# Softmax row sums taken from ScalarE's exponentials instead of from the product with the values, with one reciprocal on VectorE for two steps

## The chip, the cores and the metric

The kernel runs on one core of one Trainium2 chip. The core has five engines that work side by side, each through its own instructions in order: TensorE (PE in the profile; PEld is its loading of weights), VectorE (DVE), ScalarE (ACT), GpSimd (POOL) and SyncE (SP), which here only issues transfers. The metric is the device time of one execution in microseconds (us), smaller is better.

## What is computed

64 heads of attention (8 batches, 8 heads, 576 rows, 64 columns) in which every query keeps only its 32 largest scores, followed by a feed-forward layer with a squared ReLU on 4,608 rows of 512.

```python
scores = scale * (q @ k.T)                       # per head, 576 x 576
kth    = the 32nd largest score of each row
scores = where(scores >= kth, scores, -1e9) - max(row)
attn   = exp(scores) / (sum(exp(scores)) + 1e-9)
x      = attn @ v                                # heads side by side: 4608 x 512
h      = maximum(x @ w_in, 0)                    # 4608 x 2048
out    = (h * h) @ w_out                         # 4608 x 512
```

The sum in the denominator is what this change is about.

## The kernel before

The attention is cut into `U = 144` steps. A step `u` treats two blocks of 128 query rows (`x = 0, 1`), each against all 576 keys of its head. The loop over `u` is a software pipeline written out by hand: every instruction is pinned, so each engine runs them in the order in which the loop names them. In one pass of the loop the work of several steps is mixed:

- GpSimd finishes step `u-1`: `drop` (L409) makes a byte per score that tells whether it lies under the 32nd largest, and a transfer (L413) adds these bytes, read as huge negative numbers, to the scores `s`.
- VectorE finds the 32 largest of step `u`: `quads_of` (L323, L324), then four rounds of MAX8 (L374) with MATCH_REPLACE8 (L378) between them, and between the rounds `pairs_of(u+1)` (L314, L315), which opens the next step. Between rounds 0 and 1 stands `invert(u-4)`, a reciprocal (L475).
- TensorE makes the scores of step `u+1` (L285, banks `sc_a` and `sc_b`), the products with the values of step `u-4` (`weigh`, L461, bank `av_ps`) and pieces of the feed-forward (L579, L630).
- ScalarE, in this order: two copies of the scores of `u+1` out of PSUM (`s`, L294); now and then preparation of a coming pair of heads (L175, L213 to L225); `place(u-4)` (L494, L499), which scales the two product blocks by the reciprocals; `exps(u-2)` (L417), two exponentials of 128 x 576, with the row's maximum as bias, into `w_two`; `copy_far(u+1)` (L330); a part of the feed-forward (L586, L594 and others); and `negate(u)` (L394), which waits for the last round of MAX8 and gives GpSimd its threshold.
- SyncE transposes `w_two` with a transfer (`turn`, L426), after both exponentials of the step.

The sums come with the products: the value tile `va` has a 65th column that is all ones, so column 64 of `av_ps` is the row's sum of the weights, and `invert` reads two of them (one for each `x`) straight from PSUM. `sums(u)` gives that bank; the last two steps, 142 and 143, have banks of their own, and step 143 and half of step 142 take their weights from VectorE's `mask` and not from `exps`. Behind the loop stands the tail, which finishes steps 140 to 143 and the rest of the feed-forward.

`copy_far` and `quads_of` both touch the tile `most`; in the built program L323 of a step waits for ScalarE's L330 of the same step, and L314 waits for the second of ScalarE's two copies.

Of the kernel before, what the change touches and what calls it, by code (L numbers as in the profile page):

```python
# [13 lines left out]
f32 = mybir.dt.float32  # L14
# [4 lines left out]
AF = mybir.ActivationFunctionType  # L19
# [4 lines left out]
def kernel(  # L24
# [9 lines left out]
    nc = tc.nc  # L34
    B, H, S, D = q.shape
# [9 lines left out]
    def pin(ins):  # L45
        tc.keep_in_program_order(ins)
        return ins
# [6 lines left out]
    small = fast.enter_context(tc.tile_pool(name="small", bufs=2))  # L54
# [21 lines left out]
    w_two = [const.tile([128, 2, S], bf16, name=f"w_two_{i}") for i in "abc"]  # L76
# [185 lines left out]
    U = len(steps)  # L262
# [6 lines left out]
    st = {}  # L269
# [144 lines left out]

    def exps(u, x):
        d = st[u]
        pin(nc.scalar.activation(w_two[u % 3][:, x, 0:S], d["s"][:, x, :], AF.Exp, bias=d["neg"][:, x, 0:1]))  # L417

    def mask(u, x):
        d = st[u]  # L420
# [45 lines left out]
    def sums(u):  # L466
        if u < U - 2:
            return av
        if u not in last_two:
            last_two[u] = bank(u - (U - 2), [128, 512], f32)  # L470
        return last_two[u][:, 0:130].rearrange("p (x d) -> p x d", x=2)

    def invert(u):
        r = small.tile([128, 2, 1], f32, name="rsum", bufs=4)
        pin(nc.vector.reciprocal(r[:, :, :], sums(u)[:, :, 64:65]))  # L475
        st[u]["r"] = r
# [284 lines left out]
    def finish(w):  # L761
        if ok(w):
            invert(w)
            place(w)
# [11 lines left out]
    for u in range(U):  # L776
# [20 lines left out]
        if ok(u - 4):  # L797
            invert(u - 4)
# [11 lines left out]
        if ok(u - 2):  # L810
            exps(u - 2, 0)
            exps(u - 2, 1)
            turn(u - 2)
        fetch(4 if u < 12 else 3)
        if u == U - 1:
            early_exps(u, 0)
            early_exps(u, 1)
            exps(u - 1, 0)
# [42 lines left out]
    for x in range(2):  # L861
        turn_by_tensor(U - 1, x)
        turned(U - 1, x, False)
    one.square()
    invert(U - 4)
    place(U - 4)
    two.relu()
# [165 lines left out]
```

## Time and profile before

| | |
|---|---|
| median of 3 runs (904.73 to 907.03) | 905.09 us |
| time of the profiled execution | 905.09 us |
| its span, first to last instruction | 903.0 us |
| VectorE busy | 881.8 us, 98% |
| GpSimd busy | 779.0 us, 86% |
| ScalarE busy | 760.1 us, 84% |
| TensorE busy | 678.7 us, 75% |

The profiled execution's own time is the median itself; 2.1 us of it lie outside the span. A group of instructions is given with its line, engine, operation, output and inputs, count, busy time, mean duration of one, and the idle time of the engine before it with what ended that. Durations of neighbours on one engine overlap (the next starts before the end of the one ahead is recorded), so what an instruction takes from its engine is read from start to start. In a timeline the columns are start, duration, engine, line, operation and tiles, count, and in brackets the idle time of the engine before it and what ended that.

### The profile page before, as it was taken

To read this page: it belongs to the slowest core of one execution; us is meant where nothing else is said; L and a number is where in the kernel's file an instruction comes from. 1 tells how busy PE (TensorE), PEld (TensorE's weight loads), DVE (VectorE), ACT (ScalarE), POOL (GpSimd) and SP (SyncE) were. 2 spreads that over 40 slices of the span, in tenths; PEclk is the share of its full clock that TensorE was granted. 3 is DMA by queue.
4 is the path that set the end of the run, shared out by engine and by line. 5 is a ranking of instruction groups with operands and counts; after the bars stand their busy time and mean duration, and the time that the engine had idled before them with its cause. 6 is when DMAs were issued, how large, how long until landed. Compare 5 with 4: busy or idle time off the path is not lost.

```text
span 903.0 us, 21007 instructions
## 1 busy us (share of the span) xinstructions
PE 678.7 (75%) x6274; PEld 424.6 (47%) x6274; DVE 881.8 (98%) x3635; ACT 760.1 (84%) x1752; POOL 779.0 (86%) x818
## 2 busy tenths in 40 slices
PE   5777777777777777767687777677777777887796
PEld 3334454445444445444454444444444444554455
DVE  6999999999999999999999999999999999999995
ACT  3566799889988898888988899988999888997883
POOL 7999988988988888898898888998898988899880
PEclk9989999999999999999999999998999999999999
DMA  6699989899999999899899999999899999687762
GB/s 147 106 155 207 179 186 191 192 197 203 194 193 184 199 190 197 190 192 210 186 201 185 195 194 191 199 196 191 189 206 186 209 202 214 145 162 181 158 142 53
DMA packets 290778, 164.78 MB, mean 182 GB/s; under 512 B 258145, under 2 KB 268641, under 8 KB 290657
## 3 DMA queue, kind: packets, MB, share of 16 engines
q1 hardware_dynamic: 267408, 80.29, 48.0%
q0 software_dynamic: 21904, 82.65, 40.6%
q8 instruction: 52, 0.85, 0.4%
q14 instruction: 70, 0.57, 0.2%
q10 hardware_dynamic: 1344, 0.43, 0.2%
HBM read 37.75 MB, written 9.44 MB: 52 GB/s over the span
## 4 chain that ended last, share of the span: by engine, by line
DVE 74%; issue 12%; ACT 5%; PE 4%; DMA 2%; POOL 2%; SPq 0%; POOLq 0%; DVEq 0%; ACTq 0%
DVE m L374 31%; DVE cat L378 20%; DVE sc_b L314 6%; DVE most L315 5%; DVE cat L324 5%; DVE cat L323 5%; ACT s L294 1%; DVE rsum L475 1%; DMA s<-gone_b 1%; ACT rl L586 1%; DMA s<-gone_a 1%; POOL cat L347 1%; PE dn_ps L630 1%; PE sc_b L285 1%; ACT x_tok L494 0%
## 5 line engine op out<-in xcount | busy, mean ns | idle before, releaser
L374 DVE MAX8 m<-cat 128x8 f32<-128x104 f32 (+3 forms) x1152 | 435.4, 416 | 0.0
L378 DVE MATCH_REPLACE8 cat<-m,cat 128x104 f32<-128x104 f32 (+2 forms) x864 | 260.7, 306 | 0.0
L338 POOL TENSOR_TENSOR cat<-s 128x576 int32<-128x576 int32 (+1 forms) x144 | 238.6, 1657 | 2.7 <-ACT s L294 2.7
L347 POOL TENSOR_TENSOR cat<-cat,most 128x576 int32<-128x576 int32 (+1 forms) x144 | 196.1, 1362 | 25.0 <-DVE m L374 7.5
L285 PE MATMUL sc_b<-qkT 64*128 64x288 f32 x512 | 107.4, 494 | 88.4 <-DVE cat L324 84.2
L285 PE MATMUL sc_a<-qkT 64*128 64x288 f32 x512 | 97.3, 453 | 95.4 <-DVE most L315 39.2
L579 PEld LDWEIGHTS <-w_in 128*128 128x128 bf16 x2304 | 146.2, 101 | 38.6 <-issue 15.7
L630 PE MATMUL dn_ps<-w_out,h 128*128 128x512 bf16 x560 | 159.5, 416 | 0.3 <-ACT h L594 0.3
L579 PE MATMUL gen<-xT,w_in 128*128 128x128 bf16 x2016 | 137.1, 224 | 2.2 <-ACT xT L538 1.4
L409 POOL TENSOR_SCALAR gone_a<-s,neg 128x576 uint8<-128x576 f32 x143 | 107.1, 749 | 16.0 <-ACT neg L394 4.8
L409 POOL TENSOR_SCALAR gone_b<-s,neg 128x576 uint8<-128x576 f32 x142 | 106.3, 749 | 12.6 <-ACT neg L394 0.9
L294 ACT ACTIVATE s<-sc_b 128x576 f32<-128x576 f32 x144 | 93.4, 648 | 25.4 <-PE sc_b L285 21.5
L285 PEld LDWEIGHTS sc_a<-qkT 64*128 64x128 f32 x512 | 41.4, 186 | 123.4 <-issue 33.3
L294 ACT ACTIVATE s<-sc_a 128x576 f32<-128x576 f32 x144 | 91.3, 634 | 4.9 <-PE sc_a L285 3.2
L285 PEld LDWEIGHTS sc_b<-qkT 64*128 64x128 f32 x512 | 43.9, 198 | 103.8 <-PE av_ps L461 63.5
L394 ACT ACTIVATE neg<-m 128x4 f32<-128x4 f32 (+1 forms) x145 | 29.9, 206 | 70.6 <-DVE m L374 69.6
L594 ACT ACTIVATE h<-rl 128x512 bf16<-128x512 f32 x136 | 85.7, 630 | 4.3
L586 ACT ACTIVATE rl<-gen 128x512 f32<-128x512 f32 x142 | 83.0, 586 | 0.7 <-PE gen L579 0.6
L630 PEld LDWEIGHTS <-h 128*128 128x128 bf16 x560 | 53.3, 104 | 61.6 <-issue 26.3
L461 PEld LDWEIGHTS <-wT 128*128 128x128 bf16 (+1 forms) x1600 | 54.5, 100 | 54.4 <-issue 43.9
L413 POOL DMA_DIRECT2D s<-gone_b x67 | 59.3, 885 | 22.0 <-DVE m L374 9.0
L413 POOL DMA_DIRECT2D s<-gone_a x66 | 58.3, 884 | 20.4 <-DVE m L374 12.0
(172 smaller groups left out, 1248.6 us busy)
## 6 DMA issues: line engine op xcount, KB each, us to landing
s<-gone_b POOLq DMA_DIRECT2D x67, 576.0 KB, 4.6
s<-gone_a POOLq DMA_DIRECT2D x66, 576.0 KB, 4.8
v_raw<-in_v_dram SPq DMA_DIRECT2D x64, 128.0 KB, 3.3
k_raw<-in_k_dram SPq DMA_DIRECT2D x63, 128.0 KB, 3.4
q_raw<-in_q_dram SPq DMA_DIRECT2D x63, 128.0 KB, 3.2
out_dram<-wide SPq DMA_DIRECT2D x31, 256.0 KB, 3.0
v_raw<-in_v_dram SPq DMA_DIRECT2D x64, 32.0 KB, 3.0
w_in<-in_moe_w_in_dram POOLq DMA_DIRECT2D x8, 256.0 KB, 4.7
```

The source lines that it names most:

```text
L285: pin(nc.tensor.matmul(out=ps[j][:, x, 0:HALF], lhsT=lhsT, rhs=rhs, start=True, stop=True))
L294: pin(nc.scalar.activation(s[:, :, j * HALF:(j + 1) * HALF], ps[j][:, :, 0:HALF], AF.Copy))
L338: pin(tt(less, s[:, :, 0:wide].bitcast(i32), s[:, :, HALF:HALF + wide].bitcast(i32), op=ALU.add))
L347: pin(tt(less, less, d["most"][:, 0:n_h, :, :].bitcast(i32).rearrange("p h x n -> p x h n"), op=ALU.subtract))
L374: pin(nc.vector.max(out=m[r][:, x, :], in_=part(r, x)))
L378: pin(nc.vector.match_replace(out=part(r, x), in_to_replace=m[r][:, x, :], in_values=part(r, x), imm_value=NEG))
L409: pin(nc.gpsimd.tensor_scalar(byte[:, x, :, 1], s[:, x, :], scalar1=d["neg"][:, x, 1:2], scalar2=-HUGE, op0=ALU.add, op1=ALU.mult))
L413: pin(nc.gpsimd.dma_start(out=s[:, :, :].rearrange("p x n -> p (x n)"), in_=byte[:, :, :, :].rearrange("p x n two -> p (x n two)").bitcast ...
L579: pin(nc.tensor.matmul(out=hp[:, n * n_rows:(n + 1) * n_rows], lhsT=w_in[:, kh, (f0 + n) * 128:(f0 + n + 1) * 128], rhs=xt(kh), start=(kh ...
L586: pin(nc.scalar.activation(kept["rl"][:, :], hp, AF.Relu))
L594: pin(nc.scalar.activation(h2, flat, AF.Square))
L630: pin(nc.tensor.matmul(out=op[:, :], lhsT=held["h2"][:, f, c * 128:(c + 1) * 128], rhs=w_out[:, f, :], start=(f == 0), stop=(f == NF - 1)))
```

## The change

Each of the 284 exponentials of steps 0 to 141 also gives the sum of its 576 results, in a column of a small tile `sums` that two steps share. `invert` of an even step takes one reciprocal of the four sums of that step and of the next, from SBUF instead of PSUM, and `invert` of an odd step does nothing. Steps 142 and 143 and the tail's banks keep the old way. The column of ones and the products with it stay.

```diff
     def exps(u, x):
         d = st[u]
-        pin(nc.scalar.activation(w_two[u % 3][:, x, 0:S], d["s"][:, x, :], AF.Exp, bias=d["neg"][:, x, 0:1]))
+        if u % 2 == 0 and x == 0 and u < U - 2:
+            d["sums"] = small.tile([128, 2, 2], f32, name="sums", bufs=4)
+            st[u + 1]["sums"] = d["sums"]
+        total = d["sums"][:, u % 2, x:x + 1] if u < U - 2 else None
+        pin(nc.scalar.activation(w_two[u % 3][:, x, 0:S], d["s"][:, x, :], AF.Exp, bias=d["neg"][:, x, 0:1], accum_out=total))
...
     def invert(u):
+        if u < U - 2:
+            if u % 2 == 0:
+                both_r = small.tile([128, 2, 2, 1], f32, name="rboth", bufs=4)
+                pin(nc.vector.reciprocal(both_r[:, :, :, 0], st[u]["sums"][:, :, :]))
+                st[u]["r"], st[u + 1]["r"] = both_r[:, 0], both_r[:, 1]
+            return
         r = small.tile([128, 2, 1], f32, name="rsum", bufs=4)
         pin(nc.vector.reciprocal(r[:, :, :], sums(u)[:, :, 64:65]))
         st[u]["r"] = r
```

In the changed kernel as built, ScalarE has 284 instructions more than before, one behind each exponential that sums, and VectorE has 71 reciprocals fewer. The order of all other instructions on the five engines is the same. `place` of an odd step no longer waits for VectorE, and no reciprocal of the loop waits for TensorE.

## Prediction

> **What bounds the kernel now.** I read the engines' shares first, then the chain that ended last, then the groups of VectorE, then the waits of ScalarE. The page opens so:
>
> ```profile
> span 903.0 us, 21007 instructions
> ## 1 busy us (share of the span) xinstructions
> PE 678.7 (75%) x6274; PEld 424.6 (47%) x6274; DVE 881.8 (98%) x3635; ACT 760.1 (84%) x1752; POOL 779.0 (86%) x818
> ...
> DVE 74%; issue 12%; ACT 5%; PE 4%; DMA 2%; POOL 2%; SPq 0%; POOLq 0%; DVEq 0%; ACTq 0%
> ```
>
> VectorE is the bound: hardly idle, and most of the chain. An instruction taken from it shortens the run as long as nobody makes it wait. The engine that can is ScalarE, and it is the one that the change burdens. Its work by stretch of the run (the columns behind the stretch are its length and the busy time of PE, PEld, DVE, ACT, POOL):
>
> ```profile
> 85.00:150.00 65.00, 48.34 (x446) 30.13 (x447) 64.80 (x271) 55.58 (x130) 57.58 (x59) 0.97 0.94 188
> 150.00:300.00 150.00, 111.46 (x1058) 71.85 (x1056) 150.00 (x626) 132.21 (x309) 133.05 (x132) 0.94 0.93 194
> 300.00:450.00 150.00, 111.79 (x1069) 70.45 (x1067) 150.00 (x626) 133.30 (x309) 132.32 (x130) 0.94 0.94 195
> 450.00:600.00 150.00, 111.70 (x1049) 71.62 (x1047) 150.00 (x626) 133.41 (x308) 133.14 (x135) 0.94 0.94 194
> 600.00:780.00 180.00, 136.77 (x1297) 86.68 (x1296) 179.30 (x745) 160.50 (x374) 157.74 (x155) 0.94 0.96 196
> 780.00:815.00 35.00, 28.60 (x305) 18.45 (x304) 34.99 (x143) 33.55 (x77) 31.80 (x35) 1.00 0.77 161
> 815.00:870.00 55.00, 44.08 (x428) 27.12 (x428) 55.00 (x233) 45.98 (x103) 48.45 (x47) 0.97 0.79 166
> ```
>
> A step takes 6.00 us. Between 150 and 780 us ScalarE is idle for about 11% of it, 0.67 us a step ((630 - 559.42) / 105 steps); from 780 to 815 us only 0.25 us a step (1.45 / 5.83). Where that idle time lies, its waits tell, and one row of VectorE's own waits says that ScalarE can hold it up:
>
> ```profile
> ACT neg L394 <- DVE m L374: 69.6, 92, 3.1
> ACT s L294 <- PE sc_b L285: 21.5, 38, 1.8
> DVE cat L323 <- ACT most L330: 0.2, 1, 0.2
> ```
>
> The idle time stands before `negate` in 92 of 144 steps; in the others ScalarE is late already, and VectorE waited for it only once.
>
> **Term 1: the reciprocals that go.** VectorE loses 71 of its 142 in the loop.
>
> ```profile
> L475 DVE RECIPROCAL rsum<-av_ps 128x2 f32<-128x2 f32 x142 | 21.9, 154 | 1.3 <-PE av_ps L461 1.3
> ...
> L494 ACT ACTIVATE x_tok<-av_ps,rsum 128x64 bf16<-128x64 f32 x252 | 65.8, 321 | 1.5 <-DVE rsum L475 1.5
> ```
>
> At 154 ns each the gain would be 71 x 0.154 = 10.9 us, but neighbours overlap. The first steps have no reciprocal, so they show what one takes from the engine:
>
> ```profile
> 14.56 0.47 DVE L314 TENSOR_TENSOR sc_b<-sc_a,s 128x288 f32<-128x288 f32 x1
> 33.46 0.45 DVE L314 TENSOR_TENSOR sc_b<-sc_a,s 128x288 f32<-128x288 f32 x1
> 37.41 0.15 DVE L475 RECIPROCAL rsum<-av_ps 128x2 f32<-128x2 f32 x1
> 58.91 0.45 DVE L314 TENSOR_TENSOR sc_b<-sc_a,s 128x288 f32<-128x288 f32 x1
> ```
>
> Three steps without one take 6.30 us each ((33.46 - 14.56) / 3), the next four, the first of which holds the reciprocal shown, 6.3625 ((58.91 - 33.46) / 4). A reciprocal costs 0.0625 us, and 71 of them 71 x 0.0625 = 4.4 us. The other 71 read four sums from SBUF instead of two from PSUM. No row has that form; between nothing and twice 0.0625 it could give or take 4.4 us, and I take no difference, the rows being alike but for the source; forecast -4.4 and +4.4 both lie in the range. The Trainium skill ("Perfetto Trace Analysis", Optimizing Scalar/DVE Operations) puts VectorE's overhead at about 125 ns an instruction on PSUM and 60 on SBUF; by that the 71 that go would give 9 us and the 71 that stay 4.6 more, and the sum below would come to 907.8 us. The 0.0625 measured for one that reads PSUM disagrees, so this gets no chance of its own. The reciprocals' wait for TensorE goes with them (1.3 us in the whole run); I count nothing for it, since ScalarE's `place` there waits for the same products. The sums are ready: a step's last exponential ends a whole pass before the reciprocal that reads it, so no new wait stands on VectorE. `place` of odd steps loses its wait, worth 1.5 us in the whole run (second row), also counted at nothing. SyncE's transposes start later by what the exponentials lose; two passes lie between a transpose and its use, which covers it; without that cover each step would lose up to 0.46 us more. `negate` and the ReLUs are late with ScalarE too; behind them wait GpSimd's `drop` with its transfer and TensorE's pieces, and the transfer's reader is two passes off.
>
> **Term 2: the 284 reads on ScalarE.** Each exponential that sums is followed by an instruction that reads the sum out. No such row exists, so the price, call it c, is bounded by neighbours:
>
> ```profile
> L417 ACTq EVENT_SEMAPHORE  x141: 17/17/17, 25.7 to 879.6; - x141
> L417 ACT ACTIVATE w_two_a<-s,neg 128x576 bf16<-128x576 f32 x96 | 69.7, 786 | 2.3 <-DMA s<-gone_a 1.8 <-DMA s<-gone_b 0.4
> L394 ACT ACTIVATE neg<-m 128x4 f32<-128x4 f32 x143 | 29.5, 206 | 70.6 <-DVE m L374 69.6
> ```
>
> The least is what an entry of the queue without data takes, 0.02 us. The smallest common operation with data is `negate`: 206 ns alone, but only 0.11 from its start to its follower's (122.99 and 123.10 in the rows below). Two exponentials take 1.33 us (121.05 to 122.38), 0.665 each, although one lasts 786: 0.12 of each lies under its follower. A sum is complete only when the last element is through, so I expect the read to lose that overlap and then to take its place: c = 0.12 + 0.11 = 0.23. Pipelined like any other it is 0.11; with overlap on neither side 0.12 + 0.206 = 0.33. I take 0.23, because the read depends on the exponential ahead and nothing depends on it at once; 0.02 and 0.33 stay as ends. That is 0.46 us more of ScalarE a step, less than its mean idle time of 0.67. The same paragraph of the Trainium skill gives about 93 ns of engine time for a ScalarE instruction on SBUF; the 0.11 between starts agrees, and by 0.093 for the whole read the sum below would come to -0.6 us.
>
> **What of it reaches VectorE.** A late ScalarE is forgiven by its own idle time, and costs nothing as long as its second copy of the scores ends before L314, and L330 before L323. I carry this balance through all 144 steps of the timeline: lateness grows by 2c at each pair of exponentials, shrinks by each idle time of ScalarE, and what exceeds the margin before L314 or L323 is lost to both. One cluster in full:
>
> ```profile
> 104.99 0.21 ACT L394 ACTIVATE neg<-m 128x4 f32<-128x4 f32 x1 [1.02 <-DVE m L374]
> 106.53 0.65 ACT L294 ACTIVATE s<-sc_b 128x576 f32<-128x576 f32 x1 [0.31 <-PE gen L211]
> 108.09 1.45 ACT L417 ACTIVATE w_two_b<-s,neg 128x576 bf16<-128x576 f32 x2
> 114.07 1.45 ACT L417 ACTIVATE w_two_c<-s,neg 128x576 bf16<-128x576 f32 x2
> 119.65 0.66 ACT L294 ACTIVATE s<-sc_b 128x576 f32<-128x576 f32 x1
> 120.82 0.45 DVE L314 TENSOR_TENSOR sc_b<-sc_a,s 128x288 f32<-128x288 f32 x1
> 121.05 1.47 ACT L417 ACTIVATE w_two_a<-s,neg 128x576 bf16<-128x576 f32 x2
> 122.38 0.44 ACT L330 ACTIVATE most<-sc_b 128x288 f32<-128x288 f32 x1
> 122.87 0.44 DVE L323 TENSOR_TENSOR cat<-sc_b,most 128x288 f32<-128x288 f32 x1
> 122.99 0.21 ACT L394 ACTIVATE neg<-m 128x4 f32<-128x4 f32 x1 [0.17 <-DVE m L374]
> 123.10 0.58 ACT L586 ACTIVATE rl<-gen 128x512 f32<-128x512 f32 x1
> ```
>
> After 106.53 ScalarE never waits until 122.99. Two pairs make it 0.92 late. The copy ends at 120.31, 0.51 ahead of L314: 0.41 lost (0.47 in the balance, since VectorE is 0.06 early again by then). The third pair makes 1.38; L330 ends at 122.82, 0.05 ahead of L323: 0.92 more. Most steps have 0.8 to 1.1 us of margin at L323 and lose nothing; those in which a pair of heads is prepared lie near zero. The balance loses, with c = 0.23, 1.8 us up to 150 us, 2.1 up to 300, 2.8 up to 450, 2.2 up to 600, 4.6 up to 780, 2.3 up to 815 and nothing behind it: 15.8 us, at 54 places. In the tail the last summing pair lies ahead of the exponentials for TensorE's transposes, which wait for them:
>
> ```profile
> 881.77 0.51 PEld L443 LDWEIGHTS <-w_two_b 128*128 128x128 bf16 x9 [1.43 <-ACT w_two_b L417]
> ```
>
> so its 0.46 lands whole, 0.5. Sum: -4.4 + 15.8 + 0.5 = +11.9 us, 905.1 to 917.0 us. The profiled execution is the median itself, so nothing is to be shifted.
>
> **The rivals.**
> - *ScalarE's cover holds, and it gets faster.* With c = 0.02 the balance loses 0.5 us, with 0.05 1.6: 901.2 to 902.4 us (4.4 gained, up to 0.1 in the tail). For it speaks that on the mean the idle time covers even 0.46 us a step; against it that the margins fail step by step. It decides below c = 0.10, where the balance breaks even.
> - *The read is pipelined, no change.* c = 0.11: 4.8 us lost, 0.2 in the tail, 4.4 gained: 905.7 us. For it the 0.11 behind `negate`; against it that `negate` doesn't wait for its neighbour's last element. The 93 ns of the Trainium skill, above, would end here too.
> - *Nothing overlaps around the read.* c = 0.33: 30.9 lost and 0.7 in the tail: 932.2 us. The steps then lose as a rule, 83 of them.
> - *The saving isn't there*: the MATCH_REPLACE8 ahead of the reciprocal keeps the next MAX8 as late as the reciprocal did. Then 0 replaces -4.4: 921.4 us. Against it stand the 6.30 and 6.3625 us.
>
> **How the numbers follow.** A measurement of this kernel tells about 0.3%, 2.7 us, from no change. Forecast and costlier reads together, 0.64 (forecast 0.44, no overlap 0.14, saving absent 0.06); the pipelined read 0.19; the cover that holds 0.17. The price of the read is the largest unknown, and nothing in the trace settles it. The forecast's own range runs from c = 0.16 to 0.28, 910 to 924 us. For 8 in 10 I leave out the cheapest half of the faster case and the dearest part of the no-overlap case: 901.5 to 930. Slower 0.64, within 0.3% 0.19, faster 0.17.
>
> **What would show it.** In the changed profile: a new row of 284 on ScalarE at L421 with a duration near that of `negate`, and from the first exponential's start to L330 1.33 + 0.46 = 1.79 us; VectorE's step at 5.94 us in even and 6.00 in odd passes where it doesn't wait; a wait of L323 for L330 that has grown from 0.2 us to about 15; `negate`'s wait for L374 down from 69.6 us to under 30, and ScalarE's busy time up by some 60. I am wrong if the pair with its reads takes under 1.55 us, or if ScalarE's lateness moves its partners along, so that TensorE or GpSimd (idle 0.7 us a step between 150 and 780) runs dry first: then the loss is larger than the balance says.

## The result and the profile after

The changed kernel takes 906.82 us (median of 15 runs, 905.43 to 909.53) against 905.08 us for the kernel before in runs beside it: a ratio of 1.0022, 95% interval 1.0013 to 1.0031, that is 1.2 to 2.8 us slower. The forecast was 917.0 us.

The head of the page and the chain, in the changed kernel:

```profile
span 906.7 us, 21135 instructions
...
PE 666.8 (74%) x6197; PEld 422.1 (47%) x6274; DVE 878.3 (97%) x3564; ACT 781.8 (86%) x2036; POOL 777.1 (86%) x818
...
DVE 54%; ACT 12%; issue 12%; PE 4%; DMA 4%; POOL 3%; SPq 0%; POOLq 0%; ACTq 0%
```

VectorE is busy 3.5 us less than before and ScalarE 21.7 us more; ScalarE has gone from 5% to 12% of the chain and transfers from 2% to 4%. The new groups, by line (busy time, mean of one):

```profile
L421 ACT ACTIVATION_READ_ACCUMULATOR w_two_a<-s,neg 128x1 f32 x96 | 20.3, 212 | 0.0
L421 ACT ACTIVATION_READ_ACCUMULATOR w_two_c<-s,neg 128x1 f32 x94 | 20.1, 214 | 0.0
L421 ACT ACTIVATION_READ_ACCUMULATOR w_two_b<-s,neg 128x1 f32 x94 | 19.6, 209 | 0.0
```

The read is an instruction of its own and lasts about as long as `negate` (206 ns). What it takes from ScalarE is read from start to start:

```profile
452.90 0.78 ACT L421 ACTIVATE w_two_b<-s,neg 128x576 bf16<-128x576 f32 x1
453.57 0.21 ACT L421 ACTIVATION_READ_ACCUMULATOR w_two_b<-s,neg 128x1 f32 x1
453.66 0.78 ACT L421 ACTIVATE w_two_b<-s,neg 128x576 bf16<-128x576 f32 x1
454.33 0.20 ACT L421 ACTIVATION_READ_ACCUMULATOR w_two_b<-s,neg 128x1 f32 x1
454.42 0.41 ACT L330 ACTIVATE most<-sc_b 128x288 f32<-128x288 f32 x1
```

The read starts 0.67 us behind its exponential, as the second exponential of a pair did before (half of 1.33), and the next instruction 0.09 behind the read. The pair takes 1.52 us to L330 instead of 1.33: 0.095 us a read, not 0.23. VectorE's steps, where nothing holds them up:

```profile
450.98 0.16 DVE L481 RECIPROCAL rboth<-sums 128x4 f32<-128x4 f32 x1
453.39 0.45 DVE L314 TENSOR_TENSOR sc_b<-sc_a,s 128x288 f32<-128x288 f32 x1
459.33 0.45 DVE L314 TENSOR_TENSOR sc_b<-sc_a,s 128x288 f32<-128x288 f32 x1
462.92 0.16 DVE L481 RECIPROCAL rboth<-sums 128x4 f32<-128x4 f32 x1
465.33 0.45 DVE L314 TENSOR_TENSOR sc_b<-sc_a,s 128x288 f32<-128x288 f32 x1
```

A pass takes 5.94 us without a reciprocal and 6.00 with one. The gain is there, and the new reciprocal costs what the old one did. Where it goes, the waits of VectorE and ScalarE say (us in total, times, longest):

```profile
DVE cat L323 <- ACT most L330: 5.4, 10, 1.9
...
ACT w_two_b L421 <- DMA s<-gone_a: 5.0, 3, 2.2
ACT w_two_a L421 <- DMA s<-gone_b: 2.7, 1, 2.7
```

L323's wait for L330 has grown from 0.2 to 5.4 us. Part of it stands where the prediction's worked cluster was (the timeline around step 18):

```profile
123.64 0.81 ACT L421 ACTIVATE w_two_a<-s,neg 128x576 bf16<-128x576 f32 x1
124.31 0.23 ACT L421 ACTIVATION_READ_ACCUMULATOR w_two_a<-s,neg 128x1 f32 x1
124.40 0.44 ACT L330 ACTIVATE most<-sc_b 128x288 f32<-128x288 f32 x1
...
124.87 0.46 DVE L323 TENSOR_TENSOR cat<-sc_b,most 128x288 f32<-128x288 f32 x1 [0.56 <-ACT most L330]
```

Part stands where no step was full: an exponential waits for GpSimd's transfer, and L330 and L323 behind it (step 43):

```profile
267.07 0.90 POOL L413 DMA_DIRECT2D s<-gone_a  x1 [0.30 <-DVE cat L378]
...
274.55 0.77 ACT L421 ACTIVATE w_two_b<-s,neg 128x576 bf16<-128x576 f32 x1 [2.17 <-DMA s<-gone_a]
...
276.09 0.39 ACT L330 ACTIVATE most<-sc_b 128x288 f32<-128x288 f32 x1
...
276.50 0.46 DVE L323 TENSOR_TENSOR cat<-sc_b,most 128x288 f32<-128x288 f32 x1 [1.00 <-ACT most L330]
```

The same transfer in the kernel before: issued at 264.60, and its exponentials start at 270.04 without a wait, 5.4 us later; here 7.5 us pass (267.07 to 274.55).

```profile
264.60 0.90 POOL L413 DMA_DIRECT2D s<-gone_a  x1 [0.30 <-DVE m L374]
...
270.04 1.45 ACT L417 ACTIVATE w_two_b<-s,neg 128x576 bf16<-128x576 f32 x2
```

The transfers do not land later in the changed kernel as a rule. Their median time from issue to landing, first in the kernel before, then in the changed one:

```profile
s<-gone_a POOLq DMA_DIRECT2D x66, 576.0 KB, 4.8
...
s<-gone_a POOLq DMA_DIRECT2D x66, 576.0 KB, 4.7
```

To add the loss up, I take each step's time from L314 to L314 and count what lies above 6.00 us (5.93 in passes without a reciprocal; in the first eleven steps, above the median of those of its kind). The last three rows are runs told of below.

| profile | loss in the steps | ScalarE's waits for L413's transfers | last L314 to ScalarE's end | ScalarE's end to the span's end | span |
|---|---|---|---|---|---|
| before | 2.3 us | 6.8 us, 10 times | 25.83 us | 4.8 us | 903.0 us |
| the change | 8.4 | 10.6, 9 | 26.21 | 6.4 | 906.7 |
| the change, again | 5.1 | 11.6, 17 | 26.21 | 6.4 | 903.1 |
| before, transfers set aside | 0.7 | none | 25.85 | 4.8 | 901.6 |
| the change, transfers set aside | 2.8 | none | 26.23 | 5.1 | 898.9 |

Of the 2.3 us of the kernel before, 1.3 are two waits of a reciprocal for the PSUM bank (0.74 and 0.56 us), which the changed kernel cannot have. The fifth column shows a loss outside the steps. Behind ScalarE's last result the program only closes: the engines pass the branch around a fallback that is not taken (`tc.If`) and wait for one another. There SyncE waits for ScalarE, first in the kernel before, then in the changed one:

```profile
SPq L1028 <- ACTq L1001: 0.9, 1, 0.9
...
SPq L1038 <- ACTq L1011: 2.5, 1, 2.5
```

The wait is 2.5 us in both profiles of the change and in that of the change with L330 between the exponentials (below), and 0.7 to 1.5 us in the profiles of all other kernels of this document. Those 1.6 us lie behind all of VectorE's steps and all of L413's transfers. No run here tests where they come from; 284 more instructions on ScalarE don't bring them by themselves, since the reads alone, which have as many, show 0.9.

### The profile page after: what moved, and what is told of

It is laid out like the page before. It is cut to its first block, busy times and chain, and to the rows that moved or that the text cites. A ratio compares the mean times of both kernels' runs of the same rounds, so it can differ in the third digit from the quotient of the medians.

```text
span 906.7 us, 21135 instructions
## 1 busy us (share of the span) xinstructions
PE 666.8 (74%) x6197; PEld 422.1 (47%) x6274; DVE 878.3 (97%) x3564; ACT 781.8 (86%) x2036; POOL 777.1 (86%) x818
## 4 chain that ended last, share of the span: by engine, by line
DVE 54%; ACT 12%; issue 12%; PE 4%; DMA 4%; POOL 3%; SPq 0%; POOLq 0%; ACTq 0%
DVE m L374 22%; DVE cat L378 15%; DVE sc_b L314 5%; DVE cat L323 4%; DVE cat L324 4%; DVE most L315 4%; DMA s<-gone_a 3%; ACT s L294 2%; ACT rl L596 2%; ACT w_two_b L421 1%; ACT w_two_a L421 1%; PE sc_b L285 1%; ACT x_tok L504 1%; ACT w_two_c L421 1%; ACT most L330 1%
## 5 line engine op out<-in xcount | busy, mean ns | idle before, releaser
L338 POOL TENSOR_TENSOR cat<-s 128x576 int32<-128x576 int32 (+1 forms) x144 | 238.5, 1656 | 3.2 <-ACT s L294 3.2
L285 PE MATMUL sc_b<-qkT 64*128 64x288 f32 x512 | 104.7, 482 | 94.8 <-DVE cat L324 90.4
L640 PE MATMUL dn_ps<-w_out,h 128*128 128x512 bf16 x493 | 142.6, 409 | 7.8 <-issue 5.3
L394 ACT ACTIVATE neg<-m 128x4 f32<-128x4 f32 (+1 forms) x145 | 29.9, 206 | 57.0 <-DVE m L374 56.3
L421 ACT ACTIVATE w_two_b<-s,neg 128x576 bf16<-128x576 f32 x95 | 73.2, 784 | 6.3 <-DMA s<-gone_a 5.0
L413 POOL DMA_DIRECT2D s<-gone_b x67 | 59.2, 884 | 22.0 <-DVE m L374 13.5
```

The costliest lines, as they stand in the source:

```text
L285: pin(nc.tensor.matmul(out=ps[j][:, x, 0:HALF], lhsT=lhsT, rhs=rhs, start=True, stop=True))
L338: pin(tt(less, s[:, :, 0:wide].bitcast(i32), s[:, :, HALF:HALF + wide].bitcast(i32), op=ALU.add))
L640: pin(nc.tensor.matmul(out=op[:, :], lhsT=held["h2"][:, f, c * 128:(c + 1) * 128], rhs=w_out[:, f, :], start=(f == 0), stop=(f == NF - 1)))
```

## The experiments

Theory 1: the reads take 0.095 us each of ScalarE, and the balance of the prediction, with this price, says what reaches VectorE. Theory 2: the reads do more harm, by a loop over thresholds, GpSimd and transfers. A third, that late transfers take the gain, came after the first four runs.

### The reads alone

```diff
     def invert(u):
-        if u < U - 2:
-            if u % 2 == 0:
...
-            return
         r = small.tile([128, 2, 1], f32, name="rsum", bufs=4)
```

> The exponentials of steps 0 to 141 give their sums as in the change, but nothing reads them: all 142 reciprocals stay as before, from PSUM. Theory 1 (each read takes 0.095 us of ScalarE, as the changed profile shows, and only what the margins before L314 and L323 do not forgive reaches VectorE): the balance over the profile before gives 3.2 us lost in the steps and 0.2 in the tail, about 908.5 us. Theory 2 (the reads cost more than the balance, through late thresholds, late GpSimd transfers and exponentials that wait for these): the change lost 2.0 us while its reciprocals gave 4.4, so the reads alone cost 6.4 us, about 911.5 us.

Measured: ratio 1.0036 (1.0020 to 1.0052), 908.4 us by the ratio, 3.3 us lost (1.8 to 4.7). Theory 1 said 3.4, theory 2 6.4, which lies outside. But then the reciprocals that the change takes away are worth only 1.3 us (1.0036 - 1.0022) in its company, with an uncertainty of 1.7, where 71 passes shorter by 0.065 are worth more than 4. The closing wait of 1.6 us, which this run lacks (0.9 us here, 2.5 in the change), is about half of what is missing.

### The reciprocals alone

```diff
+    fixed = const.tile([128, 2, 2], f32, name="fixed")
+    pin(nc.gpsimd.memset(fixed[:, :, :], 32.0))
...
-                pin(nc.vector.reciprocal(both_r[:, :, :, 0], st[u]["sums"][:, :, :]))
+                pin(nc.vector.reciprocal(both_r[:, :, :, 0], fixed[:, :, :]))
```

(and no `accum_out`)

> No sums are taken; 71 reciprocals of a fixed tile of four numbers in SBUF stand where the change has them. The division by the true sums is left out. Theory 1: VectorE's gain of 71 x 0.0625 us comes through whole, 900.7 us. Rival (the gain is lost again, because ScalarE or the transfers already are as late as VectorE): 903 to 905 us.

Measured: ratio 0.9987 (0.9962 to 1.0012), median 903.59 us with runs from 900.74 to 911.59. The profile of one run has 899.7 us of span, 3.3 below the kernel before, and 5.93 us in passes without a reciprocal; its steps lose 4.0 us against 2.3. So VectorE gains what was worked out, with no read anywhere, and part is lost again. Theory 1's 4.4 us would be a ratio of 0.9951, which lies outside the interval; the rival's 903 to 905 us lies inside. In the profile ScalarE waits 7.3 us for L413's transfers and L323 2.1 us for L330. How much is lost the wide spread doesn't decide; it is what pointed to chance in something that ScalarE waits for.

### Two more reads a step

```diff
-            pin(nc.scalar.activation(s[:, :, j * HALF:(j + 1) * HALF], ps[j][:, :, 0:HALF], AF.Copy))
+            spare = small.tile([128, 1], f32, name="spare", bufs=4)
+            pin(nc.scalar.activation(s[:, :, j * HALF:(j + 1) * HALF], ps[j][:, :, 0:HALF], AF.Copy, accum_out=spare[:, :]))
```

> The change, and also a sum (which nothing uses) on the two ScalarE copies of the scores of every step, so four reads a step instead of two. Theory 1: 0.38 us of ScalarE a step; the balance loses 9.0 us against 3.8 with two, so about 5 us above the change, 912 us. Theory 2 (lateness breeds lateness over GpSimd and the transfers): well above, 916 us or more.

Measured: ratio 1.0034 (1.0019 to 1.0049), 1.1 us above the change by the ratios, with some 1.6 us of uncertainty. Theory 2, 916 us or more, falls: twice the reads don't breed lateness. Theory 1 said 5 and is too high as well, but less so than it looks: the closing wait is 1.2 us here and 2.5 in the change, so with the closing left out the distance is some 2.5 us. The steps of this profile lose 10.2 us, those of the change 8.4 and 5.1.

### One reciprocal from the bank for two steps

```diff
-    av = ps_one.tile([128, 2, 65], f32, name="av_ps")
+    av = ps_one.tile([128, 4, 65], f32, name="av_ps")
...
-            return av
+            return av[:, 2 * (u % 2):2 * (u % 2) + 2]
...
+    def invert_two(u):
+        both_r = small.tile([128, 4, 1], f32, name="rboth", bufs=4)
+        pin(nc.vector.reciprocal(both_r[:, :, :], av[:, :, 64:65]))
+        st[u - 1]["r"], st[u]["r"] = both_r[:, 0:2], both_r[:, 2:4]
...
-            invert(u - 4)
+            if u - 4 >= PAIRED:
+                invert(u - 4)
+            elif u % 2:
+                invert_two(u - 4)
...
-            place(u - 4)
+            if u - 4 >= PAIRED:
+                place(u - 4)
+            elif u % 2:
+                place(u - 5)
+                place(u - 4)
```

> From the kernel before, without any sums on ScalarE: the products of an even and an odd step lie side by side in the same PSUM bank, and for steps 0 to 119 one reciprocal of four numbers from PSUM serves both; the scaling of both steps stands in the odd pass (four blocks), none in the even one. 60 reciprocals fewer on VectorE. Theory 1: -3.75 us from VectorE; ScalarE's work is the same but for 0.4 us moved from even to odd passes, which costs 2.2 us in the balance: about 903.5 us. Rival (the margins swallow the uneven passes): 901.3 us.

Measured: ratio 0.9986 (0.9968 to 1.0004), -1.3 us, near theory 1 (-1.6); the rival's -3.8 lies outside. That the number agrees doesn't show theory 1's reason, the uneven passes: of the 4.4 us that the steps of its profile lose, 2.4 stand at step 133, where L323 waits 2.26 us for L330 behind an exponential that waited 3.54 us for its transfer. The sums were to be had in pairs without ScalarE.

### The transfers set aside

```diff
-            pin(nc.gpsimd.dma_start(out=s[:, :, :].rearrange("p x n -> p (x n)"), in_=...
+            pin(nc.gpsimd.dma_start(out=aside[u % 2][:, :], in_=...
```

> The kernel before, with GpSimd's transfers of the masks (L413) going to a tile of their own from step 9 on, at the same size and time; the exponentials no longer wait for them. The weights then are those of an unmasked softmax. Theory 3 (transfers that land late make ScalarE late at random, and eat gains): of the 2.3 us that the profile before loses in its steps about half goes, 903.5 to 904.5 us. Without it: 905 us.

> The same in the changed kernel. Theory 3: with no exponential waiting for a transfer the change is worth what the balance says at 0.095 us a read, -0.5 us against the run of the kernel before with its transfers set aside, 903 to 904 us. Theory 2 (a loss in ScalarE itself, or in the thresholds and GpSimd, beyond the balance): still 2 us above that run, 906 us.

Measured: kernel before 0.9989 (0.9977 to 1.0001), the change 0.9970 (0.9958 to 0.9982). With no exponential waiting for a transfer the change is 1.7 us faster than the kernel before treated alike (uncertainty about 1.5), where with the waits it is 2.0 us slower. Not all of these 3.7 us hang on the transfers: the closing wait of the change fell with them, from 2.5 us to 1.2, and the time behind ScalarE's end by 1.4 us, while in the kernel before both stayed. That leaves 2.3 us for the transfers, with an uncertainty of about 1.7. The profile, waits of VectorE in the changed kernel with the transfers set aside (all lines 3 higher):

```profile
DVE cat L326 <- ACT most L333: 1.3, 4, 0.6
DVE sc_b L317 <- ACT s L297: 0.6, 2, 0.3
```

ScalarE has no wait for a transfer, and the loss of 2.8 us sits mostly at steps 18, 28, 64, 106 and 126 to 129; 2.1 us of it is more than in the kernel before with its transfers aside (0.7). The balance, at 0.095 us, gave 3.7 for that difference, but on the profile before, in which late transfers hold ScalarE up too. By the same rule on the profile of the kernel before with its transfers aside it is about half as much (an estimate).

### The change once more

> The changed kernel once more. Theory 3 (chance in the landing of the transfers): about 906.8 us, a spread of some microseconds between runs, and in the profile other steps than 12, 31 and 43 lose time behind an exponential that waited for its transfer, while the losses at steps 18, 82, 102 to 107, 113 and 126 to 129, which come of ScalarE's own work, stand again. If the long losses stand at 12, 31 and 43 again, they are no chance.

Measured: ratio 1.0019 (0.9988 to 1.0050), runs from 904.88 to 912.64 us; the profile is of the fastest. In it the steps that ScalarE fills lose what they lost the first time: step 18 0.66 and 0.67 us, 102 and 106 0.30 and 0.29 the first time and 0.29 each now, 127 0.46 twice. The long losses are half and half. Steps 12 (2.05 us the first time), 31 (0.56) and 139 (0.36) lose nothing; step 13 loses 0.34; step 43 stands again, with nearly the same wait:

```profile
271.37 0.78 ACT L421 ACTIVATE w_two_b<-s,neg 128x576 bf16<-128x576 f32 x1 [2.21 <-DMA s<-gone_a]
...
273.32 0.46 DVE L323 TENSOR_TENSOR cat<-sc_b,most 128x288 f32<-128x288 f32 x1 [1.05 <-ACT most L330]
```

L323's waits behind late transfers add up to 3.7 us the first time and to 1.3 now. So it isn't all chance, but much of it changes from run to run. Why the transfer of step 43 lands late in this kernel and not in the one before stays open: nothing here tells the traffic that it shares the transfer engines with from its own issue time.

### L330 between the exponentials

```diff
         if ok(u - 2):
             exps(u - 2, 0)
-            exps(u - 2, 1)
-            turn(u - 2)
-        fetch(4 if u < 12 else 3)
...
             copy_far(u + 1)
             lesser(u + 1)
+            if ok(u - 2):
+                exps(u - 2, 1)
+                turn(u - 2)
+            fetch(4 if u < 12 else 3)
```

(the last pass keeps its order)

> The changed kernel, with copy_far(u+1) (L330) set between the two exponentials of step u-2 on ScalarE instead of behind them, and the second exponential, its read and the transpose behind it; on ScalarE and SyncE nothing else moves. L330 ends some 0.7 us earlier whenever ScalarE is late. If the loss is VectorE's wait of L323 for L330 (all theories but that of a saving that is not there), most of the 8.4 us that the changed profile's steps lose goes and the 4.4 us of the reciprocals stay: 901 to 902 us. If the saving isn't there: 905 us.

> The kernel before, with copy_far (L330) between the two exponentials; no sums on ScalarE, all reciprocals as before. Of the 2.3 us that its profile loses in the steps some 1.5 go: 903.5 us. If the gain of the changed kernel in this order came from the order alone, this one is as fast as that, 903.3 us; if the reciprocals that went are worth 4.4 us and the reads cost little in this order, it is 2 us or more behind it.

Measured: the change in this order 0.9975 (0.9964 to 0.9987), 2.3 us faster than the kernel before and 4.3 us faster than the change; the kernel before in this order 0.9995 (0.9967 to 1.0023), no different within its interval. The run of the change was expected at 901 to 902 us and came out at 903.3 by the ratio. Its steps lose 2.4 us, where the change lost 8.4 and 5.1; but from the last L314 to ScalarE's end it takes 27.1 us instead of 26.2, and the closing wait is 2.5 us. L323's wait for L330 is gone from the waits, and L314's for the copies, 2.2 us, comes next:

```profile
DVE sc_b L314 <- ACT s L294: 2.2, 5, 0.9
```

The gain of the reciprocals was there, and in the old order L323's wait for L330 took much of it (5.4 and 2.8 us in the two profiles). Two things limit this. In this order the change is 1.8 us ahead of the kernel before, with an uncertainty of 2.8, so the times by themselves don't show the gain; the steps do. And the order also spares ScalarE waits for transfers (3.4 us in 7, against 10.6 in 9) and shortens SyncE's transposes (a median of 3.7 us from issue to landing, against 4.4), so what the place of L330 does alone isn't shown.

### The reciprocals on GpSimd

```diff
-                pin(nc.vector.reciprocal(both_r[:, :, :, 0], st[u]["sums"][:, :, :]))
+                pin(nc.gpsimd.tensor_tensor(both_r[:, :, :, 0], st[u]["sums"][:, :, :], minus[:, :, :], op=ALU.pow))
```

> The kernel of the run with copy_far between the exponentials, and the 71 reciprocals of the loop on GpSimd, as a power of -1 at the end of the pass before, so VectorE has none of the 142. VectorE gains 8.9 us against the kernel before; GpSimd, idle 0.7 us a step, takes one small instruction more in two steps: 897 us. Rival: GpSimd's lateness moves to its transfers and to L347, 901 us or more.

Measured: 1.0600 (1.0575 to 1.0624), 960.98 us. The power of four numbers a row takes GpSimd 1.04 us:

```profile
L481 POOL TENSOR_TENSOR rboth<-sums,minus 128x4 f32<-128x4 f32 x71 | 74.1, 1044 | 0.0
```

On the mean that is 0.52 us a step, less than the 0.7 us that GpSimd was idle before, but those were not to be had. 0.3 us stand idle ahead of each L413 even here, and from one L338 to the next GpSimd takes 5.80 us in a pass without the power, 0.2 less than VectorE's 6.00, and 6.83 in one with it:

```profile
403.25 1.76 POOL L338 TENSOR_TENSOR cat<-s 128x576 int32<-128x576 int32 x1
...
409.06 1.74 POOL L338 TENSOR_TENSOR cat<-s 128x576 int32<-128x576 int32 x1
...
412.24 1.03 POOL L481 TENSOR_TENSOR rboth<-sums,minus 128x4 f32<-128x4 f32 x1
...
415.88 1.73 POOL L338 TENSOR_TENSOR cat<-s 128x576 int32<-128x576 int32 x1
```

So two passes take GpSimd 12.63 us: it now sets the pace (40% of the chain, VectorE 15%), and against the 12.00 of the kernel before that alone is some 45 us in 142 steps. L323 then waits 44.4 us for L330. The rival was right, and far too mild.

### Pairs from the bank, with L330 between

The kernel of the pairs from the bank, with pairs up to step 129 instead of 119 and L330 between the exponentials as above, and then with that order only up to pass 119 (the diff shows the bound and this second step):

```diff
-    PAIRED = 120
+    PAIRED = 130
...
         if ok(u - 2):
             exps(u - 2, 0)
-            if u == U - 1:
+            if u >= 120:
                 exps(u - 2, 1)
                 turn(u - 2)
...
-            if ok(u - 2):
+            if ok(u - 2) and u < 120:
                 exps(u - 2, 1)
                 turn(u - 2)
-            fetch(4 if u < 12 else 3)
+            if u < 120:
+                fetch(4 if u < 12 else 3)
```

> No sums on ScalarE: one reciprocal of four numbers from the PSUM bank for two steps, now for steps 0 to 129 (65 reciprocals fewer), and copy_far between the exponentials. -4.1 us from VectorE, no reads on ScalarE, and the order forgives the uneven passes: 901 us, ahead of both kernels. Rival: the four scalings in one pass cost what they did in the run without the order, 902.5 us.

> As the run with one reciprocal from the bank for two steps and copy_far between the exponentials, but with copy_far behind them again from pass 120 on. The order cost that run 0.65 us in the tail (26.5 us from the last L314 to ScalarE's end, against 25.85) and 1.5 us at steps 126 and 128, where the kernel before loses 0.3: 901 us. If those losses come of the uneven passes instead, nothing changes, 902.4 us.

Measured: 0.9959 (0.9931 to 0.9987), median 902.37 us; with the order only up to pass 119, 0.9926 (0.9897 to 0.9955), median 901.43 us, the fastest of all and faster than both kernels. The second ratio flatters it: six of the 17 runs of the kernel before beside it lie between 910 and 916 us; by the medians (906.12 and 901.43) it gains 4.7 us. The tail is back at 25.83 us, as expected, but of the two losses that were to go, that of step 126 is gone and that of step 128 (0.9 us) stays. Its profiled run is no better in the steps than the other, so between the two the medians (0.9 us apart) decide little.

## Why the prediction was wrong, step by step

- *The reciprocals, -4.4 us.* Right on the engine: passes without one take 5.93 to 5.94 us, the others 6.00, in every kernel that has them; 71 times 0.065 is 4.6. The sentence taken for the 71 that stay, "I take no difference", held too: a reciprocal from SBUF lasts 166 ns against 154, and its pass takes the same 6.00. The Trainium skill ("Perfetto Trace Analysis", Optimizing Scalar/DVE Operations) gives VectorE about 60 ns of overhead an instruction on SBUF and about 125 on PSUM. The steps agree with the first (0.065) and not with the second (0.0625). The reciprocals' wait for TensorE, for which the prediction counts nothing, did cost VectorE its 1.3 us in the steps before and is gone.
- *The read, c = 0.23.* Here the forecast failed. The step was "I expect the read to lose that overlap and then to take its place". The read does not wait for the exponential's last element to be recorded: it starts 0.67 us behind it, where before the next exponential started, and takes 0.095 us from start to start. The sign that the prediction named for being wrong came: the pair with its reads takes 1.52 us, under 1.55. This is the rival of the pipelined read (0.11); its time, 905.7 us, is 1.1 us under the measured 906.8. The Trainium skill ("Perfetto Trace Analysis", Optimizing Scalar/DVE Operations) gives a ScalarE instruction on SBUF about 93 ns of overhead. The trace agrees with that: 95 ns from the read's start to its follower's.
- *The balance.* With the price that was measured it loses 3.8 us and the tail 0.2, so it gives 905.1 - 4.4 + 3.8 + 0.2 = 904.7 us: the price by itself takes 12.3 us off the forecast. The measured 906.8 is 2.1 us more. 1.6 us of that are the closing wait, if every run has it as all profiles of the change do; the prediction has no term for it, and no run shows its cause. The rest, 0.5 us, is less than the interval's half width (0.8). In the steps the balance adds 3.8 to the 2.3 us of the profile before, 6.1 in all; the two profiles of the change have 8.4 and 5.1. What moves them apart is late transfers (3.7 and 1.3 us of L323's waits).
- *The transfers, put at nothing.* Here a sentence of the prediction is wrong: "the transfer's reader is two passes off" took the transfers for covered. A transfer issued in one pass is read in the next (264.60 to 270.04 in the lines above, 5.4 us), and its median landing takes 4.8. ScalarE's row in the prediction, with 1.8 us behind `gone_a` among its releasers, and the table above (6.8 us in 10 waits before) show exponentials that wait for them already. The transfers land no later on the whole in the changed kernel, but more of their lateness gets through to L323: 3.7 and 1.3 us in its two profiles, 0.2 before. Setting them aside helps the change by 2.3 us more than the kernel before, with an uncertainty of 1.7: that they cost the change more is likely, and how much isn't settled.
- *The tail, +0.5 us.* From the last L314 to ScalarE's end it grew by 0.38 us (25.83 to 26.21), in both profiles of the change: four reads at 0.095, right in kind.
- *What would show it.* The wait of L323 for L330 was named as the place, and is the place (0.2 to 5.4 us, not 15). `negate`'s wait fell from 69.6 to 56.3 us, not under 30; ScalarE's busy time rose by 21.7 us, not 60: 284 times 0.095 is 27, and the 5 us between are not accounted for.

## What to carry to other kernels

The price of a small instruction is what its follower loses from start to start, and a small neighbour on the same engine shows it; a dependence on the instruction ahead is no reason to charge the whole latency. An engine with idle time on the mean can still take the gain from the engine that bounds: look for the one instruction that the bound waits for, and put it ahead of the long work. Here that was worth 4.3 us in the changed kernel, more than the change itself, and nothing that could be measured in the kernel before. Before spending an engine's idle time, list what that time absorbs now, late transfers among it, and check from start to start whether it is idle time at all. And when two profiles are compared, compare what lies behind the last result too: here 1.6 us stood there, where the medians are 2 us apart.

## What was not expected of the hardware

A power of -1 on GpSimd takes 1.04 us for 128 x 4 numbers, against 0.17 us for VectorE's reciprocal of as many. It takes 1.03 us of GpSimd from start to start. ScalarE's read of its accumulator is a record of its own, 0.21 us long, that delays the engine by 0.095 us. The close of the program, from ScalarE's last result to the end of the span, took 4.8 us in the kernel before and 6.4 in the changed one.
